# Moving the normalisation of finished head pairs from VectorE to GpSimd in a two-attention kernel

## The chip, the cores and the metric

The kernel runs on one core of a Trainium2 chip. The metric is device time in microseconds; three runs of the kernel before gave 910.24, 911.53 and 913.7, median 911.53.

## The reference

Two attention blocks with 2048 tokens, width 512, 32 heads of 16, written side by side into one output. Block A works in four segments of 512 tokens with a causal mask inside each, and adds a memory of the earlier segments; block B is full attention. Everything is bf16.

```
# A, per segment s (L = 512):
logits = einsum('bhqd,bhkd->bhqk', qs, ks) * scale + mask
a_dot  = softmax(logits) @ vs
a_mem  = (phi(qs) @ M) / (phi(qs) @ z + 1e-6)
o      = g * a_mem + (1 - g) * a_dot          # g = sigmoid(beta), per head
M, z   = M + phi(ks)^T vs, z + sum(phi(ks))
out_A  = o @ wo
# B:
out_B  = softmax(q k^T * scale) v @ wo
```

## The kernel before

The heads come in units. One unit is every second head (parity e) of a row tile rt (8 heads) and a chunk ch of 512 queries: four heads, one in each quarter j of the partitions. The two parities of a row tile make a pair. Units of A and of B alternate.

For each block of 128 keys TensorE writes the transposed scores of the four heads into PSUM banks of 512 columns. There are two ways from there to the value product:

- ScalarE takes the banks in tiles of three and two (`s_ps`, alternating) and writes the exponential as bf16 (`pT`, L851). GpSimd zeroes what the causal mask hides in A (L861).
- VectorE takes single banks (`v_ps`, one of three spare PSUM banks) and writes them as integers whose bits, read as float16, are an approximate exponential (`vx`, L924). Three further copies with other offsets (L940, one for each further entry of LADDER) are added up in the value product, so that a weight is the sum of four such approximations. A block so treated costs VectorE four L924 and three L940, costs TensorE four value products instead of one for each head, and takes four banks from ScalarE.

The value product accumulates in one PSUM bank (`acc`). The values have columns of ones, so each head's sum of weights comes with it. When a unit is finished, VectorE transposes its bank into `tT` (L364). When both parities are there, the pair is normalised in `fin_pair`: reciprocal of the sums (L387); for B one tensor_tensor (L398) that multiplies with it and writes `tN` in bf16; for A with memory also the gate factor (`r1`, L393), the memory's denominator (`r2`, L402 and L403), then three tensor_tensor: `tT` times `r1` (L406), `aT` times `r2` (L408), their sum into `tN` (L410). A transpose of `tN` into `OT` (L412) follows, and later the output projection. The first four pairs of A have no memory and go by L393 and L398. Each tensor_tensor is 128 x 512 elements in SBUF.

What order all of this stands in is decided while the program is built. The kernel keeps a clock for each engine (`T["pe"]`, `T["act"]`, `T["dve"]`, `T["pool"]`), gives each instruction a planned duration, and appends whatever is ready: scores when ScalarE is about to need them, value products, projections as "chores" with due places, VectorE's tasks by `dve_run`, GpSimd's by `pool_run`. A block goes to VectorE (`v_pick`, `v_scores`) when VectorE's planned backlog is short enough. Products with zeros (`zero`) fill TensorE where nothing else is ready and its recent activity is low. On the chip each engine then works through its own list in that order.

A step of `fin_pair` that may go to GpSimd yields a pair: GpSimd's planned time and VectorE's. `in_turn` decides:

```
if isinstance(c, tuple):
    if T["pool"] < T["pe"] + POOLSLACK and len(ptasks) < 2:
        on[0] = nc.gpsimd
        ptasks.append((ready, c[0], step))
        return
    c = -c[1]
```

So with POOLSLACK at -99 the step goes to GpSimd only when GpSimd's planned clock lies 99 us behind TensorE's, and otherwise to VectorE. `pool_run` places a step that was put on GpSimd's list: it holds it until VectorE has at least POOLWITH (1.2 us) of tasks ready that are not marked as sharing a port with GpSimd, or until POOLWAIT (4 us) have passed.

```
free = sum(t["us"] for t in runnable() if not t["port"] and t["ready"] < T["pe"] + 0.3)
if live[0] and free < POOLWITH and T["pe"] < ptasks[0][0] + POOLWAIT:
    return
```

These conditions shape the lists alone: on the chip a GpSimd instruction starts when its inputs are there and its queue has come to it.

Of the kernel before, what the change touches and what calls it, by code (L numbers as in the profile page):

```python
# [58 lines left out]
POOLMIN = 99  # L59
TAILPV = 2  # L60
POOLTT = 1.2
POOLSLACK = -99.0
POOLWITH = 1.2
POOLWAIT = 4.0
LEAD = 2.5
# [6 lines left out]
def kernel(  # L72
# [381 lines left out]
    with ExitStack() as ms:  # L454
# [235 lines left out]
        def in_turn(g, prio, end=None):  # L690
            on = [None]

            def step():
# [7 lines left out]
# [3 lines that stand above are left out]
# [660 lines left out]
```

## Time and profile before

| | before |
|---|---|
| profiled execution | 911.53 us |
| its span in the profile | 909.7 us |
| ScalarE busy | 870.0 us (96%) |
| TensorE busy | 847.0 us (93%) |
| VectorE busy | 793.0 us (87%) |
| GpSimd busy | 154.5 us (17%) |

The span runs from the first to the last instruction. Busy time is time in which an engine executes; TensorE's includes the products with zeros. A group of instructions has its count behind "x", then busy time in us, the mean duration of one in ns, and the idle time of the engine just ahead of them, with what ended most of it. In a listing in order of time, the first column is the start in us, the second the length, and a bracket is the idle time ahead and who ended it. The window rows give the busy time and count of PE, PEld, DVE, ACT and POOL in this order, then the granted clock of TensorE, the DMA share and GB/s.

### The profile page before, as it was taken

The numbers are of one execution on the slowest core, as the hardware profiler recorded it, in microseconds if no ns is written. First come the engines' busy times: TensorE is split into PE (matmuls) and PEld (weight loads), VectorE is DVE, ScalarE is ACT, GpSimd is POOL, SyncE is SP. The second block draws the span as 40 slices with busy tenths as digits, with TensorE's granted clock in tenths as the row PEclk, the third lists the DMA queues.
The fourth block names the chain that finished last, engine by engine and source line by source line (L and its number), as shares of the span: only waits on it lengthen the run. The fifth ranks groups of instructions, "written<-read, shape, count | busy, mean of one in ns | idle before, by whom it ended". The sixth has DMA issues, their size and how long they took to land.

```text
span 909.7 us, 18814 instructions
## 1 busy us (share of the span) xinstructions
PE 847.0 (93%) x7546; PEld 261.0 (29%) x7670; DVE 793.0 (87%) x1358; ACT 870.0 (96%) x779; POOL 154.5 (17%) x328
## 2 busy tenths in 40 slices
PE   6999999999999999999999999999999999999995
PEld 2232232232332223222222232233232222222221
DVE  0766779879899999989989999998999999999994
ACT  2998999999999999999999999999999999999994
POOL 3640121330302003030120304002030300000000
PEclk7999999999999999999999999999999999999998
DMA  6800000010000110000000010000000000000000
GB/s 142 177 19 6 25 1 8 7 30 2 7 1 2 41 36 2 7 1 7 2 7 2 19 35 1 1 1 1 2 2 1 8 18 25 2 1 2 1 2 28
DMA packets 35649, 15.47 MB, mean 17 GB/s; under 512 B 27360, under 2 KB 35552, under 8 KB 35552
## 3 DMA queue, kind: packets, MB, share of 16 engines
q1 hardware_dynamic: 33280, 13.12, 6.1%
q10 hardware_dynamic: 2272, 1.05, 0.5%
q8 instruction: 62, 1.02, 0.4%
q14 instruction: 35, 0.29, 0.1%
HBM read 4.20 MB, written 4.19 MB: 9 GB/s over the span
## 4 chain that ended last, share of the span: by engine, by line
ACT 31%; PE 27%; issue 13%; DVE 7%; POOL 2%; ACTq 0%; POOLq 0%
ACT pT L851 31%; PE acc L115 13%; PE s_ps L115 8%; PE v_ps L115 4%; DVE vx L924 3%; DVE vx L940 2%; POOL pT L861 2%; PE o_ps L115 1%; ACT ex L290 1%; PE l_ps L115 0%; DVE tT L364 0%; POOL qB L265 0%; DVE osb L442 0%; PE k_ps L115 0%; DVE qc L263 0%
## 5 line engine op out<-in xcount | busy, mean ns | idle before, releaser
L851 ACT ACTIVATE pT<-s_ps 128x1536 bf16<-128x1536 f32 x749 | 858.3, 1285 | 12.9 <-PE s_ps L115 8.0
L924 DVE TENSOR_SCALAR vx<-v_ps 128x512 uint16<-128x512 f32 x496 | 326.3, 685 | 29.7 <-PE v_ps L115 24.4
L115 PE MATMUL s_ps<-qB,KB 32*128 32x512 bf16 x1552 | 249.9, 383 | 17.5 <-ACT pT L851 11.6
L940 DVE TENSOR_SCALAR vx<-vx 128x2048 uint16<-128x2048 uint16 x372 | 245.0, 691 | 2.8 <-PE v_ps L115 0.6
L115 PE MATMUL acc<-vx,VB 128*32 128x512 f16 x1984 | 182.2, 385 | 5.1 <-issue 1.8
L115 PE MATMUL v_ps<-qB,KB 32*128 32x512 bf16 x496 | 175.2, 382 | 3.4 <-issue 1.5
L861 POOL TENSOR_SCALAR_AFFINE_SELECT pT<-pT 128x256 bf16<-128x256 bf16 (+2 forms) x242 | 105.8, 465 | 288.2 <-ACT pT L851 287.1
L115 PE MATMUL acc<-pT,VB 128*32 128x512 bf16 x1552 | 153.5, 387 | 0.0
L115 PEld LDWEIGHTS <-KB 32*128 32x128 bf16 x2048 | 83.8, 91 | 238.6 <-issue 232.8
L115 PEld LDWEIGHTS <-VB 128*32 128x32 bf16 x3536 | 75.0, 94 | 163.1 <-issue 150.9
L115 PE MATMUL acc<-zeros 128*128 128x512 bf16 x324 | 110.7, 386 | 3.4 <-issue 3.3
L265 POOL TENSOR_SCALAR qA<-qc,par 128x512 bf16<-128x512 bf16 x24 | 17.4, 736 | 274.2 <-DVE qc L263 274.2
L115 PE MATMUL s_ps<-qA,kA 32*128 32x512 bf16 (+3 forms) x512 | 52.9, 303 | 6.8 <-ACT pT L851 3.8
L115 PEld LDWEIGHTS <-zeros 128*128 128x128 bf16 x429 | 34.7, 98 | 85.5 <-issue 79.9
L364 DVE STREAM_TRANSPOSE tT<-acc 128x512 f32<-128x512 f32 x64 | 44.7, 703 | 8.6 <-PE acc L115 8.2
L115 PE MATMUL acc<-pT,vA 128*32 128x128 bf16 (+3 forms) x512 | 33.3, 305 | 1.6 <-POOL pT L861 0.8
L115 PEld LDWEIGHTS <-kA 32*128 32x128 bf16 x512 | 17.6, 92 | 46.0 <-issue 42.4
L115 PE MATMUL k_ps<-xT_a,w_a 128*128 128x512 bf16 x60 | 19.6, 387 | 6.8 <-DMA xT_a<-in_A_x_dram 6.3
L265 POOL TENSOR_SCALAR qB<-qc,par 128x512 bf16<-128x512 bf16 x32 | 23.1, 734 | 7.9 <-DVE qc L263 7.9
L263 DVE CAST qc<-q_ps 128x512 bf16<-128x512 f32 x28 | 19.3, 688 | 5.0 <-PE q_ps L115 4.9
L398 POOL TENSOR_TENSOR tN<-tT,rsum 128x512 bf16<-128x512 f32 x1 | 1.1, 1055 | 130.9 <-DVE rsum L387 130.9
L442 DVE CAST osb<-o_ps 128x512 bf16<-128x512 f32 x28 | 19.1, 683 | 3.7 <-PE o_ps L115 3.7
(89 smaller groups left out, 425.3 us busy)
## 6 DMA issues: line engine op xcount, KB each, us to landing
out_dram<-osb SPq DMA_DIRECT2D x31, 128.0 KB, 1.7
w_b<-in_B_wqkv_dram SPq DMA_DIRECT2D x3, 512.0 KB, 5.3
phk<-phkT SPq DMA_TRANSPOSE x48, 2.4
w_a<-in_A_wv_dram ACTq DMA_DIRECT2D x1, 512.0 KB, 9.2
wo_a<-in_A_wo_dram SPq DMA_DIRECT2D x1, 512.0 KB, 4.3
wo_b<-in_B_wo_dram SPq DMA_DIRECT2D x1, 512.0 KB, 5.1
w_a<-in_A_wk_dram SPq DMA_DIRECT2D x1, 384.0 KB, 3.8
w_a<-in_A_wq_dram SPq DMA_DIRECT2D x1, 384.0 KB, 5.4
```

The lines of the kernel that those rows point to most:

```text
L115: return pin(nc.tensor.matmul(out, lhsT, rhs, **k))
L263: pin(nc.vector.tensor_copy(qc[:], ps[:]))
L265: pin(nc.gpsimd.tensor_scalar(dst[:, e, :], qc[:], par[:, e:e + 1], 0.0, ALU.mult, ALU.add))
L290: pin(nc.scalar.activation(ex[:], src, ACT.Exp))
L364: pin(nc.vector.transpose(st["tT"][:, e].rearrange("p c d -> p (c d)"), acc[:]))
L398: pin(eng.tensor_tensor(o, tT[:, :, :, 0:DH], rr.to_broadcast(bc), op=ALU.mult))
L442: pin(nc.vector.tensor_copy(osb[:], ps[:]))
L851: pin(nc.scalar.activation(pT[:, 0:n, :], pt[:, 0:n, :], ACT.Exp, scale=SCALE))
L861: pin(nc.gpsimd.affine_select(out=blk, in_=blk, compare_op=ALU.is_ge, fill=0.0, base=0, pattern=[[0, len(sls)], [1, P]], channel_multiplie ...
L924: pin(nc.vector.tensor_scalar(x[:, j, :], vt[:], XSCALE, float(LADDER[0]), ALU.mult, ALU.add))
L940: pin(nc.vector.tensor_scalar(p[:], x[:], float(off - LADDER[0]), 32767.0, ALU.add, ALU.min))
```

## The change

One constant of the planner. POOLSLACK goes from -99 to 1, so that a normalising tensor_tensor goes to GpSimd whenever GpSimd's planned clock is less than 1 us ahead of TensorE's and fewer than two such steps wait.

```
-POOLSLACK = -99.0
+POOLSLACK = 1.0
```

Nothing else in the text of the kernel differs. As the planner's later choices follow from its clocks, the lists of all engines differ from the third pair of A on, whose L398 is the first step that changes its engine. What is computed stays the same.

## The prediction

> **What bounds the kernel now.** I read the page's busy table first, then the groups of instructions, ScalarE's own waits, and VectorE and GpSimd side by side in time.
>
> ```profile
> span 909.7 us, 18814 instructions
> PE 847.0 (93%) x7546; PEld 261.0 (29%) x7670; DVE 793.0 (87%) x1358; ACT 870.0 (96%) x779; POOL 154.5 (17%) x328
> L851 ACT ACTIVATE pT<-s_ps 128x1536 bf16<-128x1536 f32 x749 | 858.3, 1285 | 12.9 <-PE s_ps L115 8.0
> L924 DVE TENSOR_SCALAR vx<-v_ps 128x512 uint16<-128x512 f32 x496 | 326.3, 685 | 29.7 <-PE v_ps L115 24.4
> L940 DVE TENSOR_SCALAR vx<-vx 128x2048 uint16<-128x2048 uint16 x372 | 245.0, 691 | 2.8 <-PE v_ps L115 0.6
> L115 PE MATMUL acc<-zeros 128*128 128x512 bf16 x324 | 110.7, 386 | 3.4 <-issue 3.3
> 120.00:730.00 610.00, 578.77 (x5278) 180.06 (x5362) 560.77 (x966) 606.99 (x546) 115.22 (x230) 1.00 0.03 9
> ```
>
> ScalarE sets the end: its exponentials (L851) take 858.3 us and leave 12.9 us idle before them. In the stretch from 120 to 730 us (last row, engines in the page's order) it works 606.99 of 610 us, VectorE 560.77, GpSimd 115.22. TensorE looks full, but 110.7 us of it are products with zeros (the function zero), which fill time. So a VectorE instruction saved is worth nothing by itself. It pays only through the planner, which gives the freed time to more score blocks on VectorE (L924, L940) and so takes exponentials from ScalarE.
>
> **What the plan does with the constant.** The work is laid out while the program is built, so both programs can be counted. Of the 55 tensor_tensor instructions of L398 to L410, 54 stood on VectorE before and one on GpSimd; 33 now stand on GpSimd, 32 more: 12 of L406, 9 of L408, 7 of L410, 4 of L398. VectorE gets 16 more L924 (512 for 496) and 12 more L940 (384 for 372): four more blocks of 128 keys. ScalarE loses their 16 score banks: 371 exponentials of three banks, 371 of two and one of one (1856 banks), for 374 and 375 (1872).
>
> **ScalarE, on the path.** 858.3 us over 1872 banks are 0.4585 us a bank; 16 of them are 7.3 us. This is the main term: ScalarE never waits for long, so it goes straight to the end.
>
> **VectorE, mostly beside it.** Removed: 12 x 0.641 + 9 x 0.681 + 7 x 0.690 + 2 x 0.707 + 2 x 0.690 = 21.4 us (durations by form, VectorE's groups of these lines). Added, by busy time of the groups: 16 x 326.3/496 + 12 x 245.0/372 = 10.5 + 7.9 = 18.4 us. VectorE comes out 3.0 us lighter, if nothing blocks it.
>
> **TensorE, beside it.** Sixteen s_ps products become sixteen v_ps products; acc<-pT loses 16 and acc<-vx gains 64 (four a bank instead of one): 48 x 182.2/1984 = 4.4 us more. Zero products fall by 30 net (413 to 383): 30 x 110.7/324 = 10.3 us less. TensorE is 5.9 us lighter, and its remaining filler of over 100 us hides the rest. Without that cover the 4.4 us would stand on the path.
>
> **A jam that goes.** Between 88 and 91 us the plan of before sent 28 acc<-vx products in one burst behind the last value projection of B:
>
> ```profile
> 87.28 0.61 PE L115 MATMUL acc<-vx,VB 128*32 128x512 f16 x8
> ...
> 88.74 1.26 PE L115 MATMUL acc<-vx,VB 128*32 128x512 f16 x20 [0.84 <-DVE VB L310]
> ...
> 90.64 2.37 ACT L851 ACTIVATE pT<-s_ps 128x1024 bf16<-128x1024 f32 x2 [2.27 <-PE v_ps L115]
> ```
>
> The bracket is the idle time ahead: TensorE waits 0.84 us for VB, the scores queue behind, and ScalarE stands 2.27 us, its longest stop between 30 and 890 us. In the new order the value products are spread earlier and the acc<-vx go in pieces of 4, 8 and 12 with scores between. I take 2.0 of the 2.27 us as gained. What is late next there is again ScalarE. Bounds: 2.3 gained, or 0 if another jam comes.
>
> **GpSimd, beside it, but not free.** Its one such instruction in before is a fair sample:
>
> ```profile
> 855.49 0.34 DVE L387 RECIPROCAL rsum<-tT 128x32 f32<-128x32 f32 x1
> 855.74 1.30 DVE L924 TENSOR_SCALAR vx<-v_ps 128x512 uint16<-128x512 f32 x2
> 857.07 1.29 DVE L940 TENSOR_SCALAR vx<-vx 128x2048 uint16<-128x2048 uint16 x2
> 855.91 1.05 POOL L398 TENSOR_TENSOR tN<-tT,rsum 128x512 bf16<-128x512 f32 x1 [130.92 <-DVE rsum L387]
> ```
>
> It starts 0.08 us after its reciprocal, takes 1.05 us, and two evacuations of 0.65 us run undisturbed over it. 32 more are 34 us on an engine with 755 us free; they stand behind the masks of their own unit, where GpSimd next waits for ScalarE or VectorE (gaps up to 46 us). Behind them on GpSimd's queue are the next qA and qB (L265) and masks (L861), needed later. No DMA is moved.
>
> What costs is the company. VectorE is slowed where a GpSimd instruction lies beside an L940:
>
> ```profile
> 292.76 0.65 DVE L924 TENSOR_SCALAR vx<-v_ps 128x512 uint16<-128x512 f32 x1
> 293.34 1.08 DVE L940 TENSOR_SCALAR vx<-vx 128x2048 uint16<-128x2048 uint16 x1
> 293.18 1.79 POOL L265 TENSOR_SCALAR qB<-qc,par 128x512 bf16<-128x512 bf16 x2
> ...
> 298.78 1.45 ACT L851 ACTIVATE pT<-s_ps 128x1536 bf16<-128x1536 f32 x1 [0.21 <-PE s_ps L115]
> ```
>
> The L940 takes 1.08 us instead of its median of 0.686: it lost 0.39 us under qB, and ScalarE missed 0.21 us five microseconds later. L924 beside GpSimd keeps its time.
>
> So I read the new order behind each r1 (L393) with these durations. In 7 of the 12 pairs of A whose L406 moved, VectorE's next instructions are L402 and L403 (0.18 + 0.35 us) and then an L940, which meets the rest of L406: 1.05 - 0.53 = some 0.5 us each, 3.5 us. A second meeting, of L408 or L410 with an L940, L295 or L296 behind, I find in about seven pairs, at 0.4 us (2.8 us). New waits of VectorE for GpSimd stand at 12 L412 and 5 L410; most have two or more L924 (over 1.3 us) ahead of them, but one pair has a single L244 (0.69 us) and a few others are near: 1.5 us. Behind such a wait VectorE's queue holds L924, for which TensorE's three spare PSUM banks wait. Sum: 8 us of stalls on VectorE, an estimate. Bounds: 0 (every instruction under evacuations, as in the sample) and 16 us (0.5 us at each of the 32).
>
> What of a stall reaches ScalarE? In before the collisions cost VectorE some 3 us (L940: mean 691 against median 686, 372 times, 1.9 us; L296: 17.5 us against 24 x 0.691, 0.9; L398, 0.3). From 120 to 730 us ScalarE idles 3.0 us for all reasons. So at most all; the episode above gives half, the slowed L940 at 615, 667 and 671 us (0.84, 0.89, 0.74 us) are followed by no stop. I take one third: 2.7 us, with 0 and 8 as ends.
>
> [...] If every moved instruction blocked VectorE for its whole 1.05 us, that would be 34 us of stall; by the rows two evacuations are not blocked at all, and the sum above stands without this.
>
> **The sum.** The profiled execution took 911.53 us, 1.8 around its span of 909.7, and is itself the median of the three runs. 911.5 - 7.3 - 2.0 + 2.7 = 904.9; I say 905.0 us (0.7% faster).
>
> **Rivals.** [...] *VectorE becomes the bound* (slower): where each stall comes through to ScalarE whole. With 0.5 us at each of the 32 moved instructions, 911.5 - 7.3 + 16 = 920; it decides the sign once the stall passed on exceeds 7.3/32 = 0.23 us per moved instruction. For it: VectorE is on the ending chain for 7% of the span. Against: it idles 49 us between 120 and 730. *It does little*: the planner's gain exists only in its own clock, VectorE cannot keep up with four more blocks, and ScalarE waits 5 us more for scores while the early gap closes: 911.5 - 7.3 + 5 - 1 = 908.
>
> **Chances.** Forecast 0.57; the two middle cases 0.30 together; slower 0.13. The range: low end, no stall passed and the whole jam gone plus 1 us from lighter VectorE, 901; high end, all 8 us passed and no jam gained, 912.5. Beyond it lie most of the slower case and little else. A half percent, 4.6 us, is about what a measurement of this kernel can tell from no change (its three runs spread from 910.24 to 913.7).
>
> **What would show it.** L851 busy near 851 us; L924 x512 and L940 x384; GpSimd near 188 us busy; no ScalarE stop over 1 us near 90 us; L940's mean above 700 ns; ScalarE's idle before L851 at 11 to 15 us. Wrong if that idle grows past 18 us, if L406 on GpSimd takes much over 1.05 us, or if L412 waits long for GpSimd.

## The result: slower, 921.5 us for 911.6

The changed kernel took a median of 921.54 us (919.44 to 923.28, four runs), the kernel before 911.64 beside it: ratio 1.0106, 95% interval 1.0073 to 1.0139. The forecast was 905.0, its range ended at 912.5. The page of the profiled execution (923.28 us, the longest of the four), in the lines that answer to those of before; the first line is before's own clock line, PEclk, which gives TensorE's granted clock in tenths of full speed, in 40 equal slices of the span:

```profile
PEclk7999999999999999999999999999999999999998
```

```profile
span 921.5 us, 18830 instructions
PE 852.8 (93%) x7569; PEld 261.7 (28%) x7688; DVE 801.0 (87%) x1354; ACT 864.6 (94%) x773; POOL 196.7 (21%) x360
PEclk7999999999999999999999999999987999999998
L851 ACT ACTIVATE pT<-s_ps 128x1536 bf16<-128x1536 f32 x743 | 852.6, 1279 | 27.3 <-PE s_ps L115 23.0
L924 DVE TENSOR_SCALAR vx<-v_ps 128x512 uint16<-128x512 f32 x512 | 334.8, 685 | 34.1 <-PE v_ps L115 24.2
L940 DVE TENSOR_SCALAR vx<-vx 128x2048 uint16<-128x2048 uint16 x384 | 262.9, 719 | 1.2
```

ScalarE did get its 16 banks less (852.6 us of exponentials for 858.3). But its idle time ahead of them rose from 12.9 to 27.3 us, nearly all of it waiting for scores. The rungs (the further copies, L940) take 719 ns on average for 691: over 384 of them that is 10.8 us. And the clock line, 9 or more in every middle slice of before, has an 8 and a 7 at some 690 us: TensorE ran slowly there. The three largest groups of tensor_tensor on GpSimd, 28 of the 33:

```profile
L406 POOL TENSOR_TENSOR tT<-tT,r 128x512 f32<-128x512 f32 x12 | 12.7, 1056 | 35.4 <-DVE r L393 35.4
L408 POOL TENSOR_TENSOR aT<-aT,r 128x512 f32<-128x512 f32 x9 | 11.7, 1305 | 1.0 <-DVE r L403 1.0
L410 POOL TENSOR_TENSOR tN<-tT,aT 128x512 bf16<-128x512 f32 x7 | 8.9, 1276 | 7.3 <-DVE aT L408 7.0
```

L406 takes the 1.06 us expected; L410 with two full operands 1.28; L408 takes 1.05 us four times and 1.50 to 1.51 the five times that it begins while an L940 runs.

One of the three worst places, in order of time (rows of the timeline; a bracket is idle time ahead):

```profile
679.02 1.06 POOL L406 TENSOR_TENSOR tT<-tT,r 128x512 f32<-128x512 f32 x1 [1.97 <-DVE r L393]
679.08 0.35 DVE L403 RECIPROCAL r<-r 128x32 f32<-128x32 f32 x1
679.35 1.28 DVE L940 TENSOR_SCALAR vx<-vx 128x2048 uint16<-128x2048 uint16 x1
680.04 1.51 POOL L408 TENSOR_TENSOR aT<-aT,r 128x512 f32<-128x512 f32 x1
681.62 1.27 POOL L410 TENSOR_TENSOR tN<-tT,aT 128x512 bf16<-128x512 f32 x1
681.75 1.70 DVE L940 TENSOR_SCALAR vx<-vx 128x2048 uint16<-128x2048 uint16 x1
683.50 0.40 PE L115 MATMUL acc<-vx,VB 128*32 128x512 f16 x4 [0.92 <-DVE vx L940]
684.64 0.62 PE L115 MATMUL acc<-pT,VB 128*32 128x512 bf16 x4
684.81 2.54 ACT L851 ACTIVATE pT<-s_ps 128x1536 bf16<-128x1536 f32 x2 [1.75 <-PE s_ps L115]
```

Read it downward. L406 holds the first L940 (1.28 us for 0.69); L408, begun beside that L940, takes 1.51 us for 1.05; L410 then holds the next L940 for a whole microsecond (1.70). TensorE's next product, acc<-vx, needs just that rung and stands 0.92 us, with the scores queued behind it. Then four products take 0.62 us instead of 0.40, and ScalarE waits 1.75 us. The windows around it give the clock (columns: PE, PEld, DVE, ACT, POOL busy, granted clock, DMA share, GB/s):

```profile
680.84:684.25 3.41, 2.09 (x20) 0.77 (x17) 3.41 (x5) 2.22 (x2) 1.98 (x2) 1.00 0.01 2
684.25:687.66 3.41, 3.41 (x22) 0.48 (x19) 2.69 (x5) 2.47 (x2) 0.00 (x0) 0.50 0.03 5
```

After 3.41 us in which TensorE was busy for 2.09, its clock was 0.50 until 701.3 us: a half-clock stretch. Two more begin at 302.0 (3.4 us long) and 411.2 (6.8); before had none between 30 and 900 us. That gave theory A: GpSimd's long instructions hold up L940, TensorE stops behind them, and on top its clock falls. Its rival B: four more blocks are simply too much for VectorE.

### The profile page after: what moved, and what is told of

Read it like the earlier page. It is cut to its first block, busy times and chain, and to the rows that moved or that the text cites. A ratio compares the mean times of both kernels' runs of the same rounds, so it can differ in the third digit from the quotient of the medians.

```text
span 921.5 us, 18830 instructions
## 1 busy us (share of the span) xinstructions
PE 852.8 (93%) x7569; PEld 261.7 (28%) x7688; DVE 801.0 (87%) x1354; ACT 864.6 (94%) x773; POOL 196.7 (21%) x360
## 3 DMA queue, kind: packets, MB, share of 16 engines
q10 hardware_dynamic: 2272, 1.05, 0.7%
## 5 line engine op out<-in xcount | busy, mean ns | idle before, releaser
L851 ACT ACTIVATE pT<-s_ps 128x1536 bf16<-128x1536 f32 x743 | 852.6, 1279 | 27.3 <-PE s_ps L115 23.0
L924 DVE TENSOR_SCALAR vx<-v_ps 128x512 uint16<-128x512 f32 x512 | 334.8, 685 | 34.1 <-PE v_ps L115 24.2
L115 PE MATMUL s_ps<-qB,KB 32*128 32x512 bf16 x1536 | 252.6, 388 | 17.5 <-ACT pT L851 11.1
L940 DVE TENSOR_SCALAR vx<-vx 128x2048 uint16<-128x2048 uint16 x384 | 262.9, 719 | 1.2
L115 PE MATMUL v_ps<-qB,KB 32*128 32x512 bf16 x512 | 182.1, 387 | 7.1 <-issue 3.0
L861 POOL TENSOR_SCALAR_AFFINE_SELECT pT<-pT 128x256 bf16<-128x256 bf16 (+2 forms) x242 | 108.6, 476 | 349.2 <-ACT pT L851 348.0
L115 PEld LDWEIGHTS <-VB 128*32 128x32 bf16 x3584 | 77.2, 94 | 174.4 <-issue 160.4
L115 PE MATMUL acc<-zeros 128*128 128x512 bf16 x294 | 102.2, 394 | 3.3 <-issue 3.2
L115 PE MATMUL s_ps<-qA,kA 32*128 32x384 bf16 (+3 forms) x512 | 53.7, 302 | 6.4 <-ACT pT L851 2.7
L398 POOL TENSOR_TENSOR tN<-tT,rsum 128x512 bf16<-128x512 f32 x3 | 3.5, 1162 | 122.4 <-DVE rsum L387 122.4
L442 DVE CAST osb<-o_ps 128x512 bf16<-128x512 f32 x28 | 19.2, 685 | 3.1 <-PE o_ps L115 2.9
L263 DVE CAST qc<-q_ps 128x512 bf16<-128x512 f32 x28 | 19.2, 686 | 2.5 <-PE q_ps L115 1.6
```

Source lines behind the costliest of these rows:

```text
L115: return pin(nc.tensor.matmul(out, lhsT, rhs, **k))
L263: pin(nc.vector.tensor_copy(qc[:], ps[:]))
L398: pin(eng.tensor_tensor(o, tT[:, :, :, 0:DH], rr.to_broadcast(bc), op=ALU.mult))
L442: pin(nc.vector.tensor_copy(osb[:], ps[:]))
L851: pin(nc.scalar.activation(pT[:, 0:n, :], pt[:, 0:n, :], ACT.Exp, scale=SCALE))
L861: pin(nc.gpsimd.affine_select(out=blk, in_=blk, compare_op=ALU.is_ge, fill=0.0, base=0, pattern=[[0, len(sls)], [1, P]], channel_multiplie ...
```

## The experiments

Times are medians; each ratio is against the kernel before on the same chip.

**GpSimd's steps made short.** The plan and all lists are kept; on GpSimd n is 1 of 16 columns.

```
-            pin(eng.tensor_tensor(t1, t1, rr.to_broadcast(bc), op=ALU.mult))
+            n = 1 if eng is nc.gpsimd else 16
+            pin(eng.tensor_tensor(t1[:, :, 0:n], t1[:, :, 0:n], rr[:, :, 0:n].to_broadcast([P, 2, n, DH]), op=ALU.mult))
...
```

> The lists of all engines are those of the changed kernel, but each of the 33 tensor_tensor on GpSimd works on one sixteenth of its elements (the rest of the pair is not normalised; L398 and L410 write into a tile that was zeroed at the start). Theory A (GpSimd's long instructions hold up VectorE's L940, TensorE stops behind them, its clock falls): L940 mean back from 719 to about 690 ns, no half-clock stretch between 30 and 900 us, ScalarE's idle before L851 from 27 to about 12 us, time 905 to 907 us. Rival B (four more blocks are too much for VectorE, whatever GpSimd does): time stays at 918 to 921 us and the half-clock stretches remain.

Measured: 905.16 us, ratio 0.9929 (0.9911 to 0.9946); no half-clock stretch. Of its groups of instructions:

```profile
L859 ACT ACTIVATE pT<-s_ps 128x1536 bf16<-128x1536 f32 x743 | 849.7, 1293 | 13.0 <-PE s_ps L117 10.1 <-PE v_ps L117 0.6 <-POOL pT L869 0.2
L948 DVE TENSOR_SCALAR vx<-vx 128x2048 uint16<-128x2048 uint16 x384 | 252.0, 690 | 1.2
```

L859 and L948 are L851 and L940 here. Rungs and ScalarE's idle are back at the figures of before, with the new plan. Rival B is out: VectorE carries four more blocks well, and the plan alone is worth 0.7%. All of the loss, 1.0106 against 0.9929 or some 16 us, comes with the length of GpSimd's instructions. TensorE's value products waited 4.3 us for an L940 in the changed kernel, 1.6 in before and not at all here.

**Only the sum made short.** The same edit on L410 alone.

> The same lists; only the seven L410 on GpSimd (1.28 us each) work on one sixteenth of their elements, L406 and L408 stay whole. In the changed kernel L410 held an L940 for 1.0 us at 300 and 682 us, just ahead of two of the three half-clock stretches; L406 and L408 alone stood ahead of the third, at 411 us. Theory A: the stretches at 302 and 684 us go, the one at 411 us stays; ScalarE's idle falls by some 8 us; time 912 to 915 us. If the number of GpSimd instructions matters and not which one: about 918 us (7 of 33 gone).

Measured: 911.51 us, ratio 0.9997 (0.9987 to 1.0007). The stretches at 302 and 684 us were gone, one of 3.4 us stayed at 409.5; L940's mean was 708 ns and ScalarE's idle 17.5 us. Seven of the 33 instructions carried about 10 of the 16 us, rather more than expected: which instruction an L940 meets matters more than how many there are.

**TensorE's stops filled.** Six products with zeros more, two ahead of each of the three acc<-vx that waited; VectorE, ScalarE and GpSimd keep their lists, and so the collisions stay.

```
+                if "v" in q:
+                    nvx[0] += 1
+                    if nvx[0] in (108, 171, 344):
...
+                        for _ in range(2):
+                            pin(nc.tensor.matmul(acc[:], zeros[:, 0:P], zeros[:], start=False, stop=False, ...
```

> The changed kernel with two products with zeros more on TensorE's list (0.33 us each) at each of three places: ahead of the acc<-vx that waited 0.94, 1.07 and 0.92 us for an L940 at 302, 411 and 684 us. All other lists are the same, so the collisions stay. Theory A1 (the loss comes mainly from TensorE's clock, which fell to half for 3.4, 6.8 and 17.1 us right behind these stops): the stretches go, L940 mean stays near 719 ns, ScalarE's idle falls by 8 to 10 us, time 912 to 914 us. Rival A2 (the waits themselves are the loss, the clock is a by-product): 920 us or more.

Measured: 914.07 us, ratio 1.0015 (1.0005 to 1.0026), no half-clock stretch. Rungs as slow as in the changed kernel, ScalarE's idle 18.6 for 27.3, in its groups of instructions:

```profile
L851 ACT ACTIVATE pT<-s_ps 128x1536 bf16<-128x1536 f32 x743 | 851.5, 1279 | 18.6 <-PE s_ps L115 14.9 <-PE v_ps L115 0.5 <-POOL pT L861 0.3
L940 DVE TENSOR_SCALAR vx<-vx 128x2048 uint16<-128x2048 uint16 x384 | 262.6, 717 | 1.2
```

Two microseconds of useless work, in the gaps, won back some 8 of the 16 us (1.0106 to 1.0015). So half of the loss is the clock; the other half, 1.0015 against 0.9929 or some 8 us, is TensorE's and ScalarE's plain waiting. The changed kernel's own runs agree: 919.44 and 920.06 us at mean granted clocks of 0.982 and 0.980, 923.02 and 923.28 us at 0.975. A straight line through the four, an estimate, gives 914.8 us at 0.990, the clock at which the runs with filled stops had their 914.07. The other half is less sharp. Between the profiled runs with filled stops and with short steps, ScalarE's idle time differs by 5.6 us (18.6 for 13.0) and its exponentials by 1.8 (851.5 for 849.7); a first exponential at 19.2 us for 17.3 adds 1.9 that no GpSimd step can have caused, as the first moved one comes near 60 us.

**The start held.** If GpSimd's steps start before the evacuations that the planner meant to cover them, make them start later: r1 and r2 are put on VectorE's list only when the step is placed, and the sum of A stays on VectorE. One of the places (`gate` makes r1, L393 before):

```
+            eng = (yield (POOLTT, 0.7)) or nc.vector
+            rr = gate()
+            pin(eng.tensor_tensor(t1, t1, rr.to_broadcast(bc), op=ALU.mult))
```

> The small steps that a tensor_tensor on GpSimd reads (r1; the memory's reciprocal r2) are put on VectorE's list only when the planner places that tensor_tensor, so that on the chip it starts with the bank evacuations that were meant to cover it and not some microseconds earlier; the sum of A stays on VectorE. 25 tensor_tensor stand on GpSimd, two L924 behind nearly each; the planner gives VectorE no more blocks than before (496 evacuations, 749 exponentials). Theory A: hardly a collision, L940 mean 690 to 695 ns, no half-clock stretch, time 909 to 912 us, as before. If the load on GpSimd costs wherever it stands: L940 mean above 705 ns and 914 us or more.

Measured: 921.32 us, ratio 1.0108 (1.009 to 1.0126): a miss, and of another kind. The collisions of the moved steps did go but for one rung of 1.54 us (mean 691 ns, as before), but now the consumer on VectorE comes too soon: it waits for GpSimd's tensor_tensor six times, 5.2 us in all, where before had no such wait. In its timeline L411 is L408 and L414 is L410:

```profile
742.05 1.05 POOL L411 TENSOR_TENSOR aT<-aT,r 128x512 f32<-128x512 f32 x1 [1.05 <-DVE r L410]
743.14 0.69 DVE L414 TENSOR_TENSOR tN<-tT,aT 128x512 bf16<-128x512 f32 x1 [1.17 <-POOL aT L411]
743.75 1.28 DVE L928 TENSOR_SCALAR vx<-v_ps 128x512 uint16<-128x512 f32 x2
744.48 0.94 PE L115 MATMUL o_ps<-wo_b,OT_b 128*128 128x512 bf16 x3 [1.59 <-DVE vx L928]
746.07 1.45 ACT L855 ACTIVATE pT<-s_ps 128x1536 bf16<-128x1536 f32 x1 [1.77 <-PE s_ps L115]
```

VectorE stands 1.17 us for GpSimd, TensorE 1.59 us for VectorE's evacuation, ScalarE 1.77 us; two half-clock stretches of 3.4 us (533.4 and 745.0 us) follow such places. ScalarE's idle is 18.4 us for 12.9 in before. Without the gain of the plan either, the time is that of the changed kernel; how these waits add up to all of the 10 us over before was not taken apart.

**GpSimd's steps cut into pieces.** The changed kernel with each step as two or four instructions over a part of the columns; the result is the same, as are all other lists. The cut for quarters (halves have 8 for 4), and one of the places that use it:

```
+    def cut(eng):
+        n = 4 if eng is nc.gpsimd else 16
+        return [(a, a + n) for a in range(0, 16, n)]
...
+            for a, b in cut(eng):
+                pin(eng.tensor_tensor(o[:, :, a:b], t1[:, :, a:b], t2[:, :, a:b], op=ALU.add))
...
```

> The changed kernel with each tensor_tensor on GpSimd cut into two halves (two instructions of 8 of the 16 columns each; 33 become 66); what is computed and all other lists stay the same. From 1.056 us whole and 0.241 us at a sixteenth, a half should take 0.62 us, so GpSimd gets some 6 us more work. Theory A (an L940 is held for the rest of the GpSimd instruction that it meets, then goes): the longest L940 falls from 1.70 to about 1.3 us, the mean from 719 to 700-706 ns, fewer half-clock stretches, time 910 to 915 us. Rival C (the stall goes by GpSimd's whole work, however it is cut): no better than 920 us, as GpSimd has more to do.

> The same with four quarters (132 instructions of some 0.40 us each, 1.6 us for a whole where it was 1.06). Theory A: the longest L940 about 1.1 us, mean 695 to 702 ns; but a pair's steps take half as long again on GpSimd, so VectorE may now wait for GpSimd at L410 and L412. Time 907 to 914 us. Rival C: 920 us or more.

Measured: halves 908.18 us, ratio 0.9958 (0.9943 to 0.9973); quarters 907.39 us, 0.9944 (0.9925 to 0.9962), with no half-clock stretch in either. The longest rung is 1.22 us with halves and 1.00 with quarters (1.3 and 1.1 expected), for 1.70 whole; the halves' time is better than the 910 to 915 us expected. Of the quarters:

```profile
L948 DVE TENSOR_SCALAR vx<-vx 128x2048 uint16<-128x2048 uint16 x384 | 254.3, 696 | 1.2
L415 POOL TENSOR_TENSOR aT<-aT,r 128x128 f32<-128x128 f32 x36 | 17.1, 504 | 0.0
```

A quarter takes 0.40 us undisturbed and 0.50 on average, so that a step is about twice as long on GpSimd, and yet the rungs come back from 719 to 696 ns: an L940 waits for the piece that it meets, not for the step. Both are faster than before and than the changed kernel.

**The plan starts when the chip does.** POOLWITH at 0: the planner no longer imagines that GpSimd waits for cover.

```
-POOLWITH = 1.2
+POOLWITH = 0.0
```

> POOLWITH at 0 instead of 1.2: the planner starts a GpSimd step as soon as its inputs are there, as the chip does, and its port rule then keeps L940 out of that time in the plan. 29 tensor_tensor stand on GpSimd, one block more than before on VectorE (500 evacuations for 496, 747 exponentials for 749). Theory A with the plan's error in the starting times as the cause of the collisions: L940 mean 690 to 700 ns, no half-clock stretch, time 908 to 911 us. If the collisions come from the load on GpSimd rather than from the plan's times: 914 us or more.

Measured: 907.87 us, ratio 0.9956 (0.9942 to 0.9971), no half-clock stretch, ScalarE's idle 12.1 us. The expectation held in the time (0.1 us under its range) but not in the rungs (704 ns for 690 to 700): collisions remained, six rungs of 1.28 us and more, but TensorE's longest wait for a rung was 0.45 us. VectorE waited 4.5 us at L412 for GpSimd's L410.

**VectorE late without GpSimd.** The kernel with the short steps again, but the three L940 behind which TensorE had stopped are done three times over, 1.3 us more of VectorE at each. In the kernels from here on the loads of x and phi(k) are plain copies, without the transposition, which makes the start shorter (the first exponential starts 6.7 us earlier in the control) and the numbers computed others; this one has a control of its own with the same loads. Part of the edit, with LATE = (81, 128, 258):

```
+                    for _ in range(3 if nrung[0] in LATE else 1):
+                        pin(nc.vector.tensor_scalar(p[:], x[:], float(off - LADDER[0]), 32767.0, ALU.add, ALU.min))
```

> Control for the next three, with the order of all engines as in the kernel with GpSimd's 33 steps at one sixteenth (905.2 us). Left out: the transposition in the loads of x and of phi(k), which are plain copies of the same size here, so that the numbers computed are others, with the same spread. Only the start can change, as the first loads may land sooner: 902 to 906 us, no half-clock stretch, L940 mean near 690 ns.

> The control with plain loads, in which three L940 are done three times over: the three behind which TensorE stopped in the changed kernel at 302, 411 and 684 us. VectorE is late by 1.3 us at each of three places with no long GpSimd instruction near. Theory A1 (what counts is that VectorE is late just there, and that TensorE's activity in a window of 3.41 us falls under some 0.71, which halves its clock): stops of 0.8 us and more, half-clock stretches at one to three of the places, 3 to 8 us over the control for 4 us of added work. If the lateness alone counted: at most 4 us over the control, with no stretch.

Measured: control 895.41 us for 902 to 906 expected, no stretch; with the three late rungs 903.94 us, in ten runs from 901.51 to 912.23. Against the kernel before these are 0.9815 (0.9798 to 0.9831) and 0.9917 (0.9894 to 0.994). Of the second, rows of the timeline at the first place (L951 is the rung), then the windows ahead of the other two stretches (columns as above):

```profile
288.44 2.14 DVE L951 TENSOR_SCALAR vx<-vx 128x2048 uint16<-128x2048 uint16 x3
290.63 0.40 PE L118 MATMUL acc<-vx,VB 128*32 128x512 f16 x4 [0.99 <-DVE vx L951]
293.91 1.45 ACT L860 ACTIVATE pT<-s_ps 128x1536 bf16<-128x1536 f32 x1 [1.43 <-PE s_ps L118]
```

```profile
397.60:401.00 3.40, 1.96 (x20) 0.60 (x16) 3.33 (x7) 2.92 (x4) 0.16 (x1) 0.99 0.00 0
667.20:670.60 3.40, 2.37 (x21) 0.77 (x19) 3.33 (x6) 3.08 (x3) 0.34 (x2) 1.00 0.00 0
```

All three places stopped TensorE (0.99, 1.44, 1.03 us), and a half-clock stretch followed each (at 291.7, 401.0 and 670.6 us; 3.4, 6.8 and 3.4 long). Some 4 us of VectorE's time cost 8.5 us, with GpSimd's steps at their shortest (it worked 0, 0.16 and 0.34 us in the 3.4 us ahead of the three): the second half of the chain came without a long GpSimd instruction. The ten runs spread with the clock: 901.51 us at a mean granted clock of 0.992, 902.30 to 906.09 at 0.989 to 0.984, 912.23 at 0.976.

**Both repairs at once.** POOLWITH at 0, and with it the quarters, again with plain loads.

> The kernel with POOLWITH at 0 (907.9 us), loads of x and of phi(k) plain instead of transposed, as in the control. 905 to 908 us.

> The kernel just before, with each GpSimd step also cut into four quarters (29 become 116); the lists of the other engines are the same. POOLWITH at 0 alone left L940 at a mean of 704 ns, 8 us of excess over 690. If the two repairs work on the same loss: L940 mean near 695 ns, 1 to 3 us faster than the kernel just before. If the longer GpSimd steps (1.6 us for 1.06) make VectorE wait at L412, where it already waited 4.5 us: 0 to 3 us slower.

Measured: 899.01 and 900.75 us, ratios 0.9853 (0.9837 to 0.987) and 0.9876 (0.9859 to 0.9892); the lower level is again the shorter start. The cut brought the rungs from 704 to 693 ns, 4.3 us over 375 of them, but VectorE's wait for GpSimd at the transpose behind L410 grew from 4.5 to 9.2 us:

```profile
  POOL tN L418: 9.2, 11
```

(who kept L420, here the transpose into OT, waiting: us, times; L418 is L410). So VectorE gained nothing, and the two repairs do not add. What the 1.7 us more are made of is not shown: ScalarE's idle time is the same (10.4 for 10.6 us), and 0.9 of them lie outside the span from the first to the last instruction. The kernel without the cut had one half-clock stretch of 3.4 us, at 548.7; the one with it had none.

## Why the prediction was wrong

**The plan's gain was right in its main term.** 16 banks off ScalarE: 7.3 us forecast, exponentials down by 5.7 (852.6 for 858.3) in the changed kernel and 8.6 with the short steps. The jam at 90 us went as read from the order: no ScalarE stop between 80 and 120 us above 0.15 us. But its 2.0 us did not reach the time: with the short steps ScalarE idles 13.0 us, as in before (12.9), as other stops came with the new order, the longest 1.50 us at 616 us. That was the forecast's own end "0 if another jam comes". Without collisions the sum comes to 902.2; measured with short steps, 905.2.

**The collisions were found, and under-sized.** Seven pairs where an L940 meets L406: seven rungs of 1.28 to 1.29 us, 0.6 us lost at each (0.5 forecast). About seven second meetings: seven rungs from 1.22 to 1.70 us, 0.8 us lost on average (0.4 forecast). The forecast let the second rung meet the rest of a GpSimd instruction; at the three worst places L408 begins beside the first rung and takes 1.51 us for 1.05, so that the next rung meets L408 or L410 nearly whole, and L410 takes 1.28 us and not 1.05. VectorE lost 10.8 us in rungs where 8 were expected for all, within the range given. The new waits of VectorE for GpSimd, put at 1.5 us, came to 0.3 at the transpose.

**The step that failed is "what of a stall reaches ScalarE".** I took one third, 2.7 us, with 0 and 8 as ends, though the stalls themselves were bounded by 16. What reached the time was about 16 us: plain waiting some 8 us, which is nearer three quarters of VectorE's loss, and another 8 us from TensorE's clock, which no row of before's middle showed and which the sum had no term for. The third came from small collisions: in before a rung lost 0.1 to 0.4 us, and ScalarE mostly missed nothing. At the three worst places a rung lost 0.85 to 1.0 us, and TensorE stopped for 0.92 to 1.07, because acc<-vx waits for the very rung and the scores stand behind it in the same queue. Which product comes next counts as well as the loss: behind the other eleven long rungs TensorE's longest wait for a rung was 0.67 us. Scaling the rate of small delays up to large ones was the error; "at most all" as the upper end was wrong too, since a stall can cost more than itself.

**The rivals.** "VectorE becomes the bound" named 920 us, near the 921.5 measured, but not for its reason: VectorE was no busier in share (87%) and waited as long for TensorE's banks as before (24.2 us at L924, 24.4 in before), so it did not bound the whole; three places did half of it. The point from which it decides, 0.23 us passed on at each moved instruction, was passed: 16 us over 32 are 0.5. The sign said wrong above 18 us of ScalarE idle came true at 27.3.

**How long a rung was held.** All fourteen rungs of 1.22 us or more ended 0.55 us after the GpSimd instruction that each met, whether that had taken 1.05 or up to 1.51 us, and the quarters show the wait to be one instruction long (longest rung 1.00 us for 1.70). The 34 us of stall, which the prediction counted as if each moved instruction blocked VectorE throughout, was too high, since only 14 of the 33 cost a rung half a microsecond or more.

## What to carry to other kernels

Work moved from VectorE to GpSimd was paid for here by the length of the single instruction, not by the sum: quarters, about twice the work on GpSimd, took 907.4 us where the whole steps took 921.5. So cut it, or see what the other engine has in its list at the moment when the inputs are ready, which is when it started here (the L398 of before 0.08 us after its reciprocal); and see that the consumer of the result does not then come too soon. Where one queue carries both the work that waits and the work that feeds the bound engine, look at the largest stall, not the mean. Ahead of such a wait a little filler on TensorE can be worth more than it costs (2 us of it won 8 here).

## What the runs showed of the hardware that I had not expected

TensorE's clock fell to half after windows that were merely thin. In four profiled runs the windows of 3.41 us ahead of nine half-clock stretches had TensorE busy for 53 to 71% by the profile (2.09 of 3.41 us above; 1.80 ahead of 411.2 us and 2.42 ahead of 302.0), and no stop in them was longer than 1.6 us. A tenth stretch, in the kernel with POOLWITH at 0 and plain loads, followed a window of 82%, which stays open. Windows that were not followed by one lay at 70% or above (2.39 of 3.41 us at 362.7 us with the start held); before's thinnest, the jam at 90 us, had 75% (2.57 of 3.41 us):

```profile
86.77:90.18 3.41, 2.57 (x41) 0.79 (x38) 1.31 (x3) 1.60 (x2) 0.00 (x0) 1.00 0.00 0
```

All these stretches last multiples of 3.41 us (3.4, 6.8, 17.1) and begin on one grid within a run: in the changed kernel the second and third begin 109.2 and 382.3 us after the first, 32 and 112 times 3.413 us. The runs of one kernel (the late rungs: 901.5 to 912.2 us) differ in granted clock (0.992 to 0.976), and with it in time; why they differ was not shown. A window idle for 29%, the one ahead of 302.0 us, was enough for a stretch.
